# Cluster scores of an attention kernel: from twelve split-float products per head to four plain fp32 products in column groups

## The chip, the cores and the metric

The kernel runs on one core of one Trainium2 chip. The metric is the device time of one execution in microseconds; the time before is a median of 3 runs. The engines are TensorE (PE in the rows, with PEld for its weight loads), VectorE (DVE), ScalarE (ACT), GpSimd (POOL) and SyncE (SP, which only issues transfers here; GpSimd issues transfers too).

## The reference, cut to what matters

The whole reference is an attention whose keys are masked by cluster, and behind it two mixture layers, of which the change touches nothing.

```python
q_n = q / (norm(q) + 1e-06); k_n = ...; c_n = ...       # q, k: (2, 8, 768, 64), centroids: (8, 16, 64)
q_assign = argmax(einsum('bhsd,hcd->bhsc', q_n, c_n))   # first of equal maxima
k_assign = argmax(einsum('bhsd,hcd->bhsc', k_n, c_n))
mask = q_assign[:, :, :, None] == k_assign[:, :, None, :]
scores = where(mask, matmul(q, k.T) / 8, -1e9)
attn = softmax(scores)
x = matmul(attn, v)                                     # then the two mixture layers on x
```

The cluster of a row is the centroid with the highest score among 16; the norm of the row itself doesn't matter for that.

## The kernel before, in words

There are 16 heads g (2 batches of 8), two query halves u per head, three blocks of 128 queries per half. The scores of a block are one step n. The attention is software-pipelined by slots: slot s issues the scores of step s + 4 (`S`, `s_mm`), their row maximum (`M`, `s_max`), an exponential (`E`, `s_exp`), two groups of three transposes of the probabilities of 384 queries (`T` and `t`, `transp`, L458) and their products with the values (`V` and `v`, `pv`). The order inside a slot is written out by hand:

```python
LEAD = 4
ORDER = "ESTLAtVMlvZB"
```

Everything else is put into the places `A`, `Z` and `B` of a slot by a table: `at(slot, "a", fn)` puts a function there, and `steps(base, when, gen)` runs one step of a generator at each of the places listed in `when`. "-13a" with base 6g is place A of the slot 13 before head g's slots; place A lies between the transposes `T` and `t` on TensorE. Each engine runs its own instructions strictly in the order in which this walk issues them, and waits at an instruction whose data is not there.

An operand of head g is `t1` (128 partitions, 2, 768): index j=0 are queries, j=1 keys. For j=0 partitions 0 to 63 hold the high part of the 64 features (fp32r) and 64 to 127 the low part, for j=1 the other way round, so that one product over 128 partitions gives the sum of both parts. A transfer of GpSimd fills t1 (L330), and `rest_qk` (L337, on GpSimd, one instruction for each j, 64x768) subtracts to make the low parts. Its two steps are issued at -19b and -15a for odd heads, at -19b and -15b for even ones, at -16b and -15b for head 3. Also on GpSimd are the sums and scalings of a finished pair of heads (`norm`, L552, L557, L563; a pair is finished every 12 slots, issued at 8b to 11z of the next pair), the split of the values (L351), transfers (L330, L331, L347), and the mask steps below. `t2` (80 partitions) holds the high parts again, and in rows 64 to 79 the one-hot of the cluster (for queries 0 or 1, for keys 0 or -2^60), which makes the mask part of the score product (L435).

`cluster(g)` makes these rows in 11 steps. Twelve products (L370; 128 rows of t1 stationary, 32 columns of centroids moving: 16 of their high and 16 of their low parts), the sum of both parts (L377 ScalarE, L379 VectorE), the row maximum (L381 VectorE), a difference, a scaling and a tie-break on GpSimd (L393 to L395), a second maximum (L397), a difference (L399 GpSimd), a one-hot (L401 ScalarE), six transposes of 64 columns (L405), a copy with the factor of queries or keys (L415 ScalarE) and two transfers of SyncE into t2 (L417). For heads 3 and up its steps stand at

```python
CL = ("-13a", "-13a", "-13a", "-13z", "-12z", "-12b", "-10a", "-10a", "-9a", "-9b", "-9b")
```

PSUM buffers with the tag "t" come from a ring of three banks (`ps_t`), which T, t and the cluster steps share.

Of the kernel before, what the change touches and what calls it, by code (L numbers as in the profile page):

```python
# [8 lines left out]
F32 = mybir.dt.float32  # L9
F32R = mybir.dt.float32r  # L10
BF16 = mybir.dt.bfloat16
I32 = mybir.dt.int32
U32 = mybir.dt.uint32
ACTF = mybir.ActivationFunctionType
ALU = mybir.AluOpType
AX = mybir.AxisListType
PSUM = bass.MemoryType.PSUM

B, H, S, D = 2, 8, 768, 64
NCL = 16  # L20
# [5 lines left out]
NQ = S // 128  # L26
NPAIR = H // 2
BIG = float(2.0 ** 60)
# [11 lines left out]
def tile_cluster_attention_moe(ctx, tc, qk, vt, cent, consts, wm1, wm2, probs, probs_t, out):  # L40
    nc = tc.nc
    V, A, G, T, SY = nc.vector, nc.scalar, nc.gpsimd, nc.tensor, nc.sync
# [9 lines left out]
    ident = const.tile([128, 128], F32, name="ident")  # L52
    wtie = const.tile([128, NCL], BF16, name="wtie")
    zero1 = const.tile([128, 1], F32, name="zero1")
    cT = const.tile([128, H, 2, NCL], F32R, name="cT")
    identb = const.tile([128, 128], BF16, name="identb")
# [229 lines left out]
    def attention():  # L286
        with ExitStack() as ax:
            qkp = ax.enter_context(tc.tile_pool(name="qkp", bufs=2))
            stg = ax.enter_context(tc.tile_pool(name="stg", bufs=1))
            clp = ax.enter_context(tc.tile_pool(name="clp", bufs=1))  # L290
# [4 lines left out]
            ps_t = ax.enter_context(tc.tile_pool(name="ps_t", bufs=3, space=PSUM))  # L295
            ps_v = ax.enter_context(tc.tile_pool(name="ps_v", bufs=1, space=PSUM))
# [4 lines left out]
            ops = {}  # L301
# [12 lines left out]
            def low_raw(g, j, eng):  # L314
                r = slice(64, 128) if j == 0 else slice(0, 64)
                t = ops[g]["t1"][r, j]
                eng.tensor_tensor(out=t, in0=ops[g]["raw"][j][r], in1=t.bitcast(F32), op=ALU.subtract)
# [31 lines left out]
            def rest_v(g):  # L349
                vs, vraw = ops[g]["vs"], ops[g]["vraw"]  # L350
                G.tensor_tensor(out=vs[:, :, 1], in0=vraw, in1=vs[:, :, 0].bitcast(F32), op=ALU.subtract)  # L351

            oh_t = [clp.tile([128, NQ, 2, 32], BF16, name=f"oh{h}") for h in range(2)]

            def cluster(g):


                N = 2 * NQ
                t1, t2 = ops[g]["t1"], ops[g]["t2"]
                oh = oh_t[g % 2]  # L360
                ohn = oh[:, :, :, :NCL]
                pc = (ps_v if g == 1 else ps_t).tile([128, N, 2, NCL], F32, tag="v" if g == 1 else "t", name="pc")
                sc = clp.tile([128, N, NCL], F32, tag="sc", name="sc")
                mx = clp.tile([128, N, 1], F32, tag="mx", name="mx", bufs=2)
                eq = clp.tile([128, N, NCL], BF16, tag="eq", name="eq", bufs=2)
                mw = clp.tile([128, N, 1], BF16, tag="mw", name="mw", bufs=2)
                wb = wtie.rearrange("p (o c) -> p o c", o=1).to_broadcast([128, N, NCL])
                for j in range(2):
                    for c in range(NQ):
                        T.matmul(  # L370
                            out=pc[:, 2 * c + j].rearrange("p a b -> p (a b)"),
                            lhsT=t1[:, j, c * 128:(c + 1) * 128],
                            rhs=cT[:, g % H].rearrange("p a b -> p (a b)"),
                            start=True, stop=True,
                        )
                    yield
                A.copy(out=sc, in_=pc[:, :, 1])  # L377
                yield
                V.tensor_tensor(out=sc, in0=pc[:, :, 0], in1=sc, op=ALU.add)  # L379
                yield  # L380
                V.tensor_reduce(out=mx, in_=sc, axis=AX.X, op=ALU.max)  # L381
                yield
                if g < 2:
                    V.tensor_tensor(out=eq, in0=sc, in1=mx.to_broadcast([128, N, NCL]), op=ALU.is_equal)
                    V.tensor_tensor(out=eq, in0=eq, in1=wb, op=ALU.mult)
                    yield
                    V.tensor_reduce(out=mw, in_=eq, axis=AX.X, op=ALU.max)
                    yield
                    V.tensor_tensor(
                        out=ohn, in0=eq.rearrange("p (c j) n -> p c j n", j=2),  # L390
                        in1=mw.rearrange("p (c j) n -> p c j n", j=2).to_broadcast([128, NQ, 2, NCL]), op=ALU.is_equal)
                else:
                    G.tensor_tensor(out=sc, in0=sc, in1=mx.to_broadcast([128, N, NCL]), op=ALU.subtract)  # L393
                    G.tensor_tensor(out=sc, in0=sc, in1=huge.rearrange("p (o c) -> p o c", o=1).to_broadcast([128, N, NCL]), op=ALU.mult)
                    G.tensor_tensor(out=sc, in0=sc, in1=wb, op=ALU.add)  # L395
                    yield
                    V.tensor_reduce(out=mx, in_=sc, axis=AX.X, op=ALU.max)  # L397
                    yield
                    G.tensor_tensor(out=sc, in0=sc, in1=mx.to_broadcast([128, N, NCL]), op=ALU.subtract)  # L399
                    yield  # L400
                    A.activation(out=ohn, in_=sc.rearrange("p (c j) n -> p c j n", j=2), func=ACTF.Relu, bias=1.0)  # L401
                yield
                pt = ps_t.tile([64, S], BF16, tag="t", name="pt")
                for c in range(NQ):
                    T.transpose(pt[:, c * 128:(c + 1) * 128], oh[:, c].rearrange("p j n -> p (j n)"), identb)  # L405
                yield
                if g < 3:
                    A.activation(out=t2[64:80, 1], in_=pt[32:48], func=ACTF.Copy, scale=BIG, bias=-BIG)
                    yield
                    for hs in (slice(0, 384), slice(384, S)):  # L410
                        A.copy(out=t2[64:80, 0, hs], in_=pt[0:16, hs])  # L411
                    yield
                else:
                    mk = clp.tile([64, S], F32, tag="mk", name="mk")
                    A.activation(out=mk, in_=pt, func=ACTF.Identity, scale=mkc[:, 0:1], bias=mkc[:, 1:2])  # L415
                    for j in range(2):
                        SY.dma_start(out=t2[64:80, j].bitcast(F32), in_=mk[32 * j:32 * j + 16])  # L417
                    yield

            P_t, rs_t, nm_t, pT, pv_t, xu_t, r_t = {}, {}, {}, {}, {}, {}, {}  # L420

# [148 lines left out]
            def at(slot, pos, fn):  # L570
                tasks.setdefault((slot, pos), []).append(fn)

            def steps(base, when, gen):
                for w in when:
                    at(min(base + int(w[:-1]), NS - 1), w[-1], lambda: next(gen, None))
# [5 lines left out]
            def lazy(make, *args):  # L581
                yield from make(*args)
# [5 lines left out]
            V.memset(zero1, 0.0)  # L588
            huge = clp.tile([128, 1], F32, name="huge")
            V.memset(huge, HUGE)  # L590
            mkc = clp.tile([64, 2], F32, name="mkc")
            for j, v in enumerate((1.0, 0.0, BIG, -BIG)):
                V.memset(mkc[j // 2 * 32:j // 2 * 32 + 32, j % 2:j % 2 + 1], v)

            def warm(n):

# [8 lines left out]
            load_raw(1)  # L605
            load_raw(2)
            setup, head = consts_setup(clp, ps_t), cluster(0)
            warm(11)
            next(setup)
# [47 lines left out]
            for p in range(P - 1):  # L657
                steps(12 * (p + 1), ("1a", "2z", "2b", "5a"), recip(p))
                steps(12 * (p + 1), ("8b", "9z", "10a", "10z", "11z"), norm(p, G))
            CL = ("-13a", "-13a", "-13a", "-13z", "-12z", "-12b", "-10a", "-10a", "-9a", "-9b", "-9b")  # L660
            CL1 = ("-3a", "-3z", "-3b", "-2z", "-2b", "-1z", "-1z", "0z", "0b", "1a")
            CL2 = ("-10a", "-10a", "-10a", "-10z", "-9a", "-9a", "-8a", "-8a", "-8b", "-7z", "-7b", "-6a")
            steps(0, CL1, head)
            at(-1, "z", hold)
            for j in range(2):
                at(-1, "b", lambda j=j: low_raw(2, j, G))
            for g in range(NH):
                c = 6 * g
                if g > 3:
                    at(c - 23, "z", lambda g=g: load_qk(g))  # L670
                if g > 2:
                    steps(c, ("-16b", "-15b") if g == 3 else ("-19b", "-15a") if g % 2 else ("-19b", "-15b"), lazy(rest_qk, g, G))
                if g > 1:
                    steps(c, CL2 if g == 2 else CL, lazy(cluster, g))
                if g:
                    at(0 if g == 1 else c - 8, "z", lambda g=g: load_v(g))
                at(c - 4, "z", lambda g=g: rest_v(g))
# [16 lines left out]
            for slot in range(-LEAD, NS):  # L694
                n = slot + LEAD
                ready = slot >= 0
                if ready:
                    u, t = divmod(slot, 3)
# [41 lines left out]
    ct = {}  # L740
# [614 lines left out]
    with tc.manual_schedule():  # L1355
        attention()
        moe()
# [46 lines left out]
```

## Time and profile before

| | |
|---|---|
| median of 3 runs | 1037.88 us (1036.76 to 1038.18) |
| profiled execution | 1037.56 us, of which the span from first to last instruction is 1035.5 us |
| granted TensorE clock, mean | 0.995 of 2.4 GHz |
| attention stage | about 16 to 266 us of the span |
| busy share | PE 99%, PEld 81%, DVE 81%, ACT 61%, POOL 34% |

The profile is of one execution. A row of the timeline gives start and duration in us, the engine, the line, the operation, output and inputs, the count of equal instructions merged, and in brackets how long the engine was idle before it and what ended the wait. Matmuls are pipelined, so that a row's duration is longer than the time until the next one starts.

### The profile page before, as it was taken

The page shows a single profiled execution, that of the slowest core. Times are in us where ns is not written, and L with a number is a line of the kernel's source. Part 1 is how long each engine was busy: PE and PEld are TensorE (multiplying, and loading weights), DVE is VectorE, ACT ScalarE, POOL GpSimd, SP SyncE. Part 2 cuts the span into 40 slices and gives each one's busy share as a digit, 9 for nine tenths or more (in the row PEclk, how much of TensorE's full clock was granted, in tenths as well). Part 3 has the DMA queues.
Part 4 walks back from the last instruction along what each step waited for, and adds up shares of the span by engine and source line. Part 5 has one row for each costly group of instructions (what it writes and reads, how often), then busy time and mean ns, then how long its engine had stood idle before and what let it go on. Part 6 is the DMA issues. An engine that isn't in the chain of part 4 may idle for free.

```text
span 1035.5 us, 14784 instructions
## 1 busy us (share of the span) xinstructions
PE 1025.4 (99%) x5051; PEld 841.4 (81%) x5051; DVE 836.5 (81%) x1528; ACT 626.9 (61%) x1200; POOL 349.6 (34%) x395
## 2 busy tenths in 40 slices
PE   8999999999999999999999999999999999999998
PEld 5788888887788888788888888888888888888887
DVE  6788888898678887878687688898888888888875
ACT  6778878777467565645545656565555646555550
POOL 2747777652200101010100144433344443334430
PEclk8999999999999999999999999999999999999999
DMA  8677868832632624262410176755667665555753
GB/s 207 166 170 179 189 156 170 184 77 56 175 85 82 142 82 102 81 143 77 107 42 21 41 143 122 157 108 103 122 132 153 122 138 110 124 117 122 143 102 122
DMA packets 61267, 126.23 MB, mean 122 GB/s; under 512 B 15648, under 2 KB 20256, under 8 KB 61192
## 3 DMA queue, kind: packets, MB, share of 16 engines
q0 software_dynamic: 35632, 62.93, 33.1%
q1 hardware_dynamic: 25272, 62.30, 20.3%
q8 instruction: 39, 0.64, 0.3%
q14 instruction: 36, 0.29, 0.1%
q10 hardware_dynamic: 288, 0.07, 0.0%
HBM read 69.47 MB, written 3.21 MB: 70 GB/s over the span
## 4 chain that ended last, share of the span: by engine, by line
PE 95%; DVE 2%; ACT 2%; issue 0%; DMA 0%; SPq 0%; ACTq 0%; DVEq 0%
PE pa L900 19%; PE pb L275 14%; PE pd L1127 13%; PE pd L1253 9%; PE pb L1182 7%; PE ps L458 6%; PE ps L435 4%; PE pb L900 3%; PE ps L436 3%; PE pa L275 3%; PE pv L488 2%; PE pv L493 2%; PE pv L494 2%; PE pc L370 2%; PE pd L1297 2%; PE pu L275 1%
## 5 line engine op out<-in xcount | busy, mean ns | idle before, releaser
L1145 POOL DMA_DIRECT2D acc<-ev x84 | 74.1, 1019 | 169.1 <-ACT ev L1144 165.6
L441 DVE CUSTOM_DVE_ANT_0 junk<-ps,zero 128x768 bf16<-128x768 f32 x96 | 91.0, 948 | 14.4 <-PE ps L436 11.9
L452 ACT ACTIVATE P<-ps,nm 128x768 f32<-128x768 f32 x96 | 86.7, 903 | 12.4 <-DVE nm L441 12.1
L1259 POOL DMA_DIRECT2D acc<-ev x24 | 20.6, 858 | 202.0 <-ACT ev L1258 199.3
L275 PE MATMUL pb<-xh,wuh 128*128 128x512 f32 x216 | 85.4, 396 | 0.0
L275 PE MATMUL pb<-xh,wul 128*128 128x512 f32 x216 | 84.9, 393 | 0.0
L275 PE MATMUL pb<-xl,wuh 128*128 128x512 f32 x216 | 84.1, 389 | 0.0
L458 PE MATMUL ps<-ident,P 128*128 128x128 f32 x576 | 82.7, 275 | 0.0
L1138 DVE TENSOR_TENSOR acc<-pd,acc 128x512 f32<-128x512 f32 x112 | 75.5, 689 | 8.5 <-PE pd L1127 5.0
L477 DVE TENSOR_TENSOR lo<-ps,hi 128x384 fp32r<-128x384 f32 x128 | 69.3, 554 | 15.2 <-ACT hi L463 14.1
L1153 POOL DMA_DIRECT2D acc<-ev x56 | 48.6, 868 | 86.1 <-ACT ev L1152 47.8
L1012 ACT CAST hh<-snap 128x512 fp32r<-128x512 f32 x31 | 19.3, 622 | 94.5 <-DVE snap L1009 94.5
L435 PE MATMUL ps<-t 80*128 80x512 f32 x192 | 70.4, 367 | 1.4 <-ACT t L411 0.8
L463 ACT CAST hi<-ps 128x384 fp32r<-128x384 f32 x128 | 57.3, 479 | 21.1 <-PE ps L458 20.9
L458 PEld LDWEIGHTS ps<-ident,P 128*128 128x128 f32 x576 | 65.6, 141 | 1.4
L436 PE MATMUL ps<-t 128*128 128x512 f32 x192 | 62.2, 345 | 0.0
L900 PE MATMUL pa<-xsh,wuh 128*128 128x512 f32 x150 | 59.7, 398 | 0.1
L1152 ACT ACTIVATE ev<-pb,pn 128x512 f32<-128x512 f32 x56 | 38.5, 687 | 34.8 <-PE pb L1182 23.4
L900 PE MATMUL pa<-xsh,wul 128*128 128x512 f32 x150 | 59.0, 393 | 0.0
L900 PE MATMUL pa<-xsl,wuh 128*128 128x512 f32 x150 | 58.9, 393 | 0.0
L900 PE MATMUL pa<-xh,wuh 128*128 128x512 f32 x150 | 58.4, 390 | 0.0
L900 PE MATMUL pa<-xh,wul 128*128 128x512 f32 x150 | 58.4, 389 | 0.0
(276 smaller groups left out, 3136.5 us busy)
## 6 DMA issues: line engine op xcount, KB each, us to landing
acc<-ev POOLq DMA_DIRECT2D x164, 256.0 KB, 4.6
wraw<-in_wm SPq DMA_DIRECT2D x68, 512.0 KB, 3.8
t<-in_qk POOLq DMA_DIRECT2D x13, 768.0 KB, 6.3
t<-in_qk POOLq DMA_DIRECT2D x14, 384.0 KB, 7.8
raw<-in_qk SPq DMA_DIRECT2D x26, 192.0 KB, 7.0
x<-x SPq DMA_DIRECT2D x21, 192.0 KB, 2.8
R<-rd SPq DMA_DIRECT2D x16, 192.0 KB, 3.4
out<-acc SPq DMA_DIRECT2D x11, 256.0 KB, 2.0
```

The source lines that it names most:

```text
L275: T.matmul(out=ps, lhsT=w[:, o:o + 128], rhs=x, start=(k == 0 and m == 0), stop=(k == 3 and m == 2))
L435: T.matmul(out=ps, lhsT=t2[:, 0, qs], rhs=t2[:, 1, ks], start=True, stop=False)
L436: T.matmul(out=ps, lhsT=t1[:, 0, qs], rhs=t1[:, 1, ks], start=False, stop=True)
L441: V.tensor_tensor_reduce(out=junk, in0=S_t[n], in1=zero1.to_broadcast([128, S]), scale=-0.125, scalar=3.0e38, op0=ALU.add, op1=ALU.min, ac ...
L452: A.activation(out=P_t[n], in_=S_t.pop(n), func=ACTF.Exp, scale=0.125, bias=nm_t.pop(n), accum_out=rs_t[p][:, h, c:c + 1])
L458: T.transpose(ps[:, i * 128:(i + 1) * 128], P_t[3 * u + i][:, j * 128:(j + 1) * 128], ident)
L900: T.matmul(out=ps, lhsT=w[:, o:o + 128], rhs=r, start=first and i == 0 and m == 0, stop=i == 1 and m == 2, skip_group_check=not first)
L1127: T.matmul(out=ps[s], lhsT=w[i][:, o + s * 128:o + s * 128 + 128], rhs=x[j], start=first and m == 0, stop=m == 2, skip_group_check=not first)
L1138: V.tensor_tensor(out=y, in0=ps, in1=y, op=ALU.add)
L1145: G.dma_start(out=acc1[:, 2 * half + s, tb * 512:(tb + 1) * 512], in_=ev, accum_op=ALU.add)
L1182: T.matmul(out=ps, lhsT=h[i][:, f, ts_], rhs=w[j][:, f * DM + cs.start:f * DM + cs.stop], start=(f == 0 and m == 0), stop=(f == FC - 1 and ...
L1253: T.matmul(out=ps, lhsT=w[:, o:o + 128], rhs=x[:, f, sl], start=(n == 0), stop=(n == len(terms) - 1))
```

## The change

Heads 3 to 15 get a function of their own, `cluster4`. At its start the centroids stand still, 32 columns of them (16 of the head and 16 of a neighbour, which are dropped later), and four plain fp32 products of 384 moving columns write four groups of 32 partitions of one bank: queries and keys of the first and of the second half. Each plain fp32 product takes the sum of both parts of the centroids, which GpSimd adds once, in slot 2. ScalarE copies the scores (128x384), three fp32 transposes turn them, ScalarE copies the 16 wanted columns of each block, and from there the steps are those of before (`best`). The one-hots are turned in three transposes of 128 columns instead of six of 64; the mask copy is 128x384 instead of 64x768, and four transfers of 16x384 replace two of 16x768. The steps start one slot earlier: the products at -14a, the copy at -14z, transposes and second copy at -13a; from -12z on the places are the old ones. Heads 0 to 2 keep the products of before.

```diff
+            def best(g, sc):
+                oh = oh_t[g % 2]
+                mx = clp.tile([128, N2, 1], F32, tag="mx", name="mx", bufs=2)
+                V.tensor_reduce(out=mx, in_=sc, axis=AX.X, op=ALU.max)
+                yield
...
+                A.activation(out=oh[:, :, :, :NCL], in_=sc.rearrange("p (c j) n -> p c j n", j=2), func=ACTF.Relu, bias=1.0)
+                yield
...
+            def cluster4(g):
+                t1, t2 = ops[g]["t1"], ops[g]["t2"]
+                pc = ps_t.tile([128, 384], F32, tag="t", name="pc")
+                o = max(g % H - 1, 0) * NCL
+                cF = ct["cn"][:, o:o + 32]
+                o = g % H * NCL - o
+                for i in range(4):
+                    half, j = divmod(i, 2)
+                    T.matmul(out=pc[32 * i:32 * i + 32], lhsT=cF, rhs=t1[:, j, half * 384:half * 384 + 384].bitcast(F32),
+                             start=True, stop=True, skip_group_check=True)
+                yield
+                cs = clp.tile([128, 384], F32, tag="cs", name="cs")
+                A.copy(out=cs, in_=pc)
+                yield
+                ps = ps_t.tile([128, 384], F32, tag="t", name="pcT")
+                for c in range(3):
+                    T.transpose(ps[:, c * 128:(c + 1) * 128], cs[:, c * 128:(c + 1) * 128], ident)
+                yield
+                sc = clp.tile([128, N2, NCL], F32, tag="sc", name="sc")
+                A.copy(out=sc, in_=ps.rearrange("p (n c) -> p n c", c=32)[:, :, o:o + NCL])
+                yield
+                yield from best(g, sc)
+                pt = ps_t.tile([128, 384], BF16, tag="t", name="pt")
+                for c in range(3):
+                    T.transpose(pt[:, c * 128:(c + 1) * 128], oh_t[g % 2][:, 2 * c:2 * c + 2].rearrange("p i j n -> p (i j n)"), identb)
+                yield
+                mk = clp.tile([128, 384], F32, tag="mk", name="mk")
+                A.activation(out=mk, in_=pt, func=ACTF.Identity, scale=mkc[:, 0:1], bias=mkc[:, 1:2])
+                for i in range(4):
+                    half, j = divmod(i, 2)
+                    SY.dma_start(out=t2[64:80, j, half * 384:half * 384 + 384].bitcast(F32), in_=mk[32 * i:32 * i + 16])
+                yield
...
-            mkc = clp.tile([64, 2], F32, name="mkc")
-            for j, v in enumerate((1.0, 0.0, BIG, -BIG)):
-                V.memset(mkc[j // 2 * 32:j // 2 * 32 + 32, j % 2:j % 2 + 1], v)
+            mkc = clp.tile([128, 2], F32, name="mkc")
+            for i in range(4):
+                for j in range(2):
+                    G.memset(mkc[32 * i:32 * i + 32, j:j + 1], ((1.0, 0.0), (BIG, -BIG))[i % 2][j])
...
-            CL = ("-13a", "-13a", "-13a", "-13z", "-12z", "-12b", "-10a", "-10a", "-9a", "-9b", "-9b")
+            CL = ("-14a", "-14z", "-13a", "-13a", "-12z", "-12b", "-10a", "-10a", "-9a", "-9b", "-9b")
...
+            at(2, "z", lambda: G.tensor_tensor(out=ct["cn"].rearrange("p (h c) -> p h c", h=H), in0=cT[:, :, 0].bitcast(F32), in1=cT[:, :, 1].bitcast(F32), op=ALU.add))
...
-                    steps(c, CL2 if g == 2 else CL, lazy(cluster, g))
+                    steps(c, *((CL2, lazy(cluster, g)) if g == 2 else (CL, lazy(cluster4, g))))
```

## Rows read from the trace of the kernel before

**Rows 1.** The page: busy time by engine, and the chain that ended last.

```profile
PE 1025.4 (99%) x5051; PEld 841.4 (81%) x5051; DVE 836.5 (81%) x1528; ACT 626.9 (61%) x1200; POOL 349.6 (34%) x395
...
PE 95%; DVE 2%; ACT 2%; issue 0%; DMA 0%; SPq 0%; ACTq 0%; DVEq 0%
```

**Rows 2.** Timeline of TensorE, 109 to 116 us (start us, us, engine, line).

```profile
109.84 0.54 PE L488 MATMUL pv<-hi,vn 128*64 128x384 f32 x1
109.84 0.54 PE L488 MATMUL pv<-pT,vn 128*64 128x384 f32 x1
...
110.53 0.50 PE L405 MATMUL pt<-identb,oh 128*64 128x128 bf16 x6
110.96 0.50 PE L435 MATMUL ps<-t 80*128 80x512 f32 x1
...
111.77 0.82 PE L458 MATMUL ps<-ident,P 128*128 128x128 f32 x6
112.35 0.42 PE L493 MATMUL pv<-hi,vs 128*128 128x384 f32 x1
...
114.09 1.49 PE L370 MATMUL pc<-cT,t 128*128 128x32 f32 x12
115.43 0.55 PE L458 MATMUL ps<-ident,P 128*128 128x128 f32 x3
```

**Rows 3.** Timeline of TensorE's weight loads, at head 3's products and at 110 us.

```profile
37.52 1.41 PEld L370 LDWEIGHTS pc<-cT,t 128*128 128x128 f32 x12 [0.17 <-POOL t L337]
...
109.83 0.13 PEld L488 LDWEIGHTS pv<-hi,vn 128*64 128x64 f32 x1 [0.17 <-issue]
```

**Rows 4.** Groups of instructions of ScalarE (busy us, mean ns, idle before), 26 to 250 us.

```profile
L463 ACT CAST hi<-ps 128x384 fp32r<-128x384 f32 x118 | 52.8, 479 | 16.9 <-PE ps L458 16.7 <-ACT hi L463 0.2
...
L415 ACT ACTIVATE mk<-pt,mkc 64x768 f32<-64x768 bf16 x13 | 12.9, 993 | 3.7 <-PE pt L405 3.7
```

**Rows 5.** Timeline of GpSimd: second L337 of heads 3, 6, 7, 8, 14; first mask step.

```profile
35.68 1.84 POOL L337 TENSOR_TENSOR t<-raw,t 64x768 fp32r<-64x768 f32 x1
...
82.25 1.85 POOL L337 TENSOR_TENSOR t<-raw,t 64x768 fp32r<-64x768 f32 x1
...
93.62 1.82 POOL L337 TENSOR_TENSOR t<-raw,t 64x768 fp32r<-64x768 f32 x1
...
104.68 0.52 POOL L393 TENSOR_TENSOR sc<-sc,mx 128x192 f32<-128x192 f32 x1 [3.13 <-DVE mx L381]
...
112.45 1.84 POOL L337 TENSOR_TENSOR t<-raw,t 64x768 fp32r<-64x768 f32 x1
...
203.05 1.84 POOL L337 TENSOR_TENSOR t<-raw,t 64x768 fp32r<-64x768 f32 x1
```

**Rows 6.** Timeline of VectorE: the row maximum of head 7's cluster scores.

```profile
104.17 0.34 DVE L381 TENSOR_REDUCE mx<-sc 128x12 f32<-128x192 f32 x1
```

**Rows 7.** Timeline of TensorE: transposes at -14 of five heads; head 6's first scores.

```profile
35.03 0.82 PE L458 MATMUL ps<-ident,P 128*128 128x128 f32 x6
...
81.47 0.82 PE L458 MATMUL ps<-ident,P 128*128 128x128 f32 x6
...
96.28 0.82 PE L458 MATMUL ps<-ident,P 128*128 128x128 f32 x6
...
106.31 0.39 PE L435 MATMUL ps<-t 80*128 80x512 f32 x1
...
141.97 0.82 PE L458 MATMUL ps<-ident,P 128*128 128x128 f32 x6
...
202.37 0.82 PE L458 MATMUL ps<-ident,P 128*128 128x128 f32 x6
```

**Rows 8.** Timeline of SyncE's queue: the two mask transfers of head 6.

```profile
96.59 1.19 SPq L417 DMA_DIRECT2D t<-mk  x2
```

**Rows 9.** All mask transfers (L417): from issue to landing.

```profile
DMA to landing us min/median/max: 2.1/3.4/6.7
```

**Rows 10.** One stretch: busy us by engine (instructions), PE clock, DMA share, GB/s.

```profile
193.00:196.50 3.50, 2.72 (x15) 1.76 (x15) 2.89 (x7) 3.29 (x9) 1.06 (x3) 1.00 0.69 174
```

More of the change, by code (lines that the diff above doesn't have):

```diff
@@ L351, in rest_v @@
                 G.tensor_tensor(out=vs[:, :, 1], in0=vraw, in1=vs[:, :, 0].bitcast(F32), op=ALU.subtract)
+            N2 = 2 * NQ
+            wb = wtie.rearrange("p (o c) -> p o c", o=1).to_broadcast([128, N2, NCL])
             oh_t = [clp.tile([128, NQ, 2, 32], BF16, name=f"oh{h}") for h in range(2)]
+            def best(g, sc):
[3 more added lines that the diff above has]
+                yield
+                G.tensor_tensor(out=sc, in0=sc, in1=mx.to_broadcast([128, N2, NCL]), op=ALU.subtract)
+                G.tensor_tensor(out=sc, in0=sc, in1=huge.rearrange("p (o c) -> p o c", o=1).to_broadcast([128, N2, NCL]), op=ALU.mult)
+                G.tensor_tensor(out=sc, in0=sc, in1=wb, op=ALU.add)
+                yield
+                V.tensor_reduce(out=mx, in_=sc, axis=AX.X, op=ALU.max)
+                yield
+                G.tensor_tensor(out=sc, in0=sc, in1=mx.to_broadcast([128, N2, NCL]), op=ALU.subtract)
+                yield
+                A.activation(out=oh[:, :, :, :NCL], in_=sc.rearrange("p (c j) n -> p c j n", j=2), func=ACTF.Relu, bias=1.0)
+                yield
             def cluster(g):
-                N = 2 * NQ
                 t1, t2 = ops[g]["t1"], ops[g]["t2"]
@@ L361, in cluster @@
                 ohn = oh[:, :, :, :NCL]
[L362 to L367, printed above, removed]
+                pc = (ps_v if g == 1 else ps_t).tile([128, N2, 2, NCL], F32, tag="v" if g == 1 else "t", name="pc")
+                sc = clp.tile([128, N2, NCL], F32, tag="sc", name="sc")
                 for j in range(2):
@@ L380, in cluster @@
                 yield
-                V.tensor_reduce(out=mx, in_=sc, axis=AX.X, op=ALU.max)
-                yield
                 if g < 2:
-                    V.tensor_tensor(out=eq, in0=sc, in1=mx.to_broadcast([128, N, NCL]), op=ALU.is_equal)
+                    mx = clp.tile([128, N2, 1], F32, tag="mx", name="mx", bufs=2)
+                    eq = clp.tile([128, N2, NCL], BF16, tag="eq", name="eq", bufs=2)
+                    mw = clp.tile([128, N2, 1], BF16, tag="mw", name="mw", bufs=2)
+                    V.tensor_reduce(out=mx, in_=sc, axis=AX.X, op=ALU.max)
+                    yield
+                    V.tensor_tensor(out=eq, in0=sc, in1=mx.to_broadcast([128, N2, NCL]), op=ALU.is_equal)
                     V.tensor_tensor(out=eq, in0=eq, in1=wb, op=ALU.mult)
@@ L391, in cluster @@
                         in1=mw.rearrange("p (c j) n -> p c j n", j=2).to_broadcast([128, NQ, 2, NCL]), op=ALU.is_equal)
+                    yield
                 else:
[L393 to L402, printed above, removed]
+                    yield from best(g, sc)
                 pt = ps_t.tile([64, S], BF16, tag="t", name="pt")
@@ L406, in cluster @@
                 yield
[L407 to L418, printed above, removed]
+                A.activation(out=t2[64:80, 1], in_=pt[32:48], func=ACTF.Copy, scale=BIG, bias=-BIG)
@@ new lines, in cluster @@
+                yield
+                for hs in (slice(0, 384), slice(384, S)):
+                    A.copy(out=t2[64:80, 0, hs], in_=pt[0:16, hs])
+                yield
+            def cluster4(g):
[8 more added lines that the diff above has]
+                             start=True, stop=True, skip_group_check=True)
+                yield
+                cs = clp.tile([128, 384], F32, tag="cs", name="cs")
+                A.copy(out=cs, in_=pc)
+                yield
+                ps = ps_t.tile([128, 384], F32, tag="t", name="pcT")
+                for c in range(3):
+                    T.transpose(ps[:, c * 128:(c + 1) * 128], cs[:, c * 128:(c + 1) * 128], ident)
+                yield
+                sc = clp.tile([128, N2, NCL], F32, tag="sc", name="sc")
+                A.copy(out=sc, in_=ps.rearrange("p (n c) -> p n c", c=32)[:, :, o:o + NCL])
+                yield
+                yield from best(g, sc)
+                pt = ps_t.tile([128, 384], BF16, tag="t", name="pt")
+                for c in range(3):
+                    T.transpose(pt[:, c * 128:(c + 1) * 128], oh_t[g % 2][:, 2 * c:2 * c + 2].rearrange("p i j n -> p (i j n)"), identb)
+                yield
+                mk = clp.tile([128, 384], F32, tag="mk", name="mk")
[3 more added lines that the diff above has]
+                    SY.dma_start(out=t2[64:80, j, half * 384:half * 384 + 384].bitcast(F32), in_=mk[32 * i:32 * i + 16])
+                yield
```

## Prediction, made before the change was run

> **What bounds the kernel now.** I read the page first: TensorE is busy for 99% of the span, and 95% of the chain that ended last is TensorE's [rows 1]. So a microsecond taken from TensorE's stream counts, and so does a microsecond for which it is made to wait; work on the other engines counts only through such waits. Then I read TensorE's timeline in the attention stage, where the change lies, to see what the old products and turns take from one start to the next, which is their price on the bound engine [rows 2], and its weight loads, which show what the next product waited for [rows 3]. Last I read GpSimd's timeline over the same slots, since GpSimd finishes the operand that the moved products read [rows 5].
>
> **What is removed from TensorE.** The old scores of one head are 12 products. In the slot read here the first starts at 114.09 and the transposes behind them at 115.43, so they hold TensorE for 1.34 us. The six one-hot turns go from 110.53 to 110.96, 0.43 us [rows 2]. Together 1.77 us for each of 13 heads.
>
> **What is added to TensorE.** The four fp32 products with 32 stationary columns have no row of their own. The nearest are the two fp32 products of 384 columns with 64 stationary columns (L488), which write different halves of the output's partitions. Both start at 109.84, and what follows starts at 110.53 [rows 2], so two groups ran side by side in 0.69 us. Ahead of them the weight load stood 0.17 us for "issue" [rows 3]. From below: four groups side by side and no entry gap, 0.69 us. From above: four in a row, 4 x 0.69 + 0.17 = 2.93 us. I take 0.86 us, four side by side with the gap, since the row shows groups running together and nothing in it ties that to two.
> The Trainium skill (TensorE: Matmul & The Clock Gate, Part 3, "Measured speedup vs the span model") speaks a little against this: three column tiles of 32 gave a speedup of 2.38, not 3, so a pack costs more than one product. By that figure, as an estimate, 3 / 2.38 = 1.26 times 0.69 us is 0.87 us, with the gap 1.04 us, and the end of the sum below would be 2.3 us later. The trace of before has only two tiles (L488) and can't decide it.
> The three fp32 transposes of the scores go by L458, six of which go from 111.77 to 112.35 [rows 2], 0.097 us each: 0.29 us. The three bf16 one-hot turns go at the old 0.43 / 6 = 0.072 us each: 0.22 us; should a stationary side twice as wide make them as dear as the fp32 ones, 0.29 us.
> New sum: 0.86 + 0.29 + 0.22 = 1.37 us against 1.77, so 0.40 us less per head and **5.2 us less in 13 heads**, if nothing waits.
>
> **What the other engines get.** ScalarE loses half of the mask copy (0.99 us for 768 columns) and gains a copy of 128x384, which by L463 is 0.48 us [rows 4]: even. VectorE loses an addition. SyncE issues four mask transfers instead of two: the two took 1.19 us to issue from 96.59 [rows 8], so two more make it about 2.4 us, to 99.0; with the longest landing seen, 6.7 us [rows 9], that is 105.7, and the first scores of that head (6) start at 106.31 [rows 7]. So it is hidden, by only 0.6 us in the worst landing and by some 4 in the usual one; were it late, scores would wait by that much. Behind these issues on SyncE stand the loads of the next values and operands, about 1.2 us later, which are asked for several slots ahead. GpSimd's one extra addition (slot 2) stands in a stretch in which it waits for a transfer; the small sets of the constants move to GpSimd before anything there is due. Both at nothing; if the cover is gone, well under 1 us, once. The three-bank ring gets one allocation more per head, but the turned scores' bank waits only for a ScalarE copy issued a whole slot before.
>
> **What is moved, and this decides.** The products go from -13a to -14a, one slot earlier. Their rows come from t1, and the half of t1 for the keys is finished by the second L337 of the head on GpSimd. For even heads this L337 is issued at -15b, just ahead. But it does not run then, since GpSimd is behind its program there: it waits for the first row maximum of the odd head before (VectorE, starting at 104.17 [rows 6]), and then runs without a break from 104.68 through mask steps, operand transfers, the value split and the sums of the finished pair, with L337 the last, 112.45 to 114.29 [rows 5]. In the old kernel the key half was first read 0.67 us after 114.09, that is at 114.76: 0.47 us to spare. At -14a it is wanted a slot earlier. The transposes of that slot start at 111.77 [rows 2], and three of them later, at 112.06, the new products come. The second product (keys, first half) then waits until 114.29: **2.23 us**. TensorE takes its products in order, so behind it stand the other two products, three transposes, the value products and the next scores; ScalarE and VectorE then run dry.
> This falls on every even head whose L337 stands behind the sums of a pair, which are heads 6, 8, 10, 12 and 14, five in all. For the first, L337 ends at 84.10 [rows 5] and the place is 81.47 + 0.29 = 81.76 [rows 7]: 2.34 us. For the last, 204.89 against 202.37 + 0.29: 2.23 us. With 2.22 for each of the other two: **11.2 us**. Head 4 has no pair ahead of it.
> Odd heads have L337 two positions earlier and behind no sums: head 7's ends at 95.44 [rows 5], and its place is 96.28 + 0.29 = 96.57 [rows 7], 1.1 us to spare, so they get no wait.
> Head 3 has both halves late: its L337 runs 35.68 to 37.52 [rows 5], and the old products waited 0.17 us for it [rows 3]. The new place is 35.03 + 0.29 = 35.32 [rows 7]: 2.20 us, 2.0 of them new.
> Does the wait heal itself? No: the next one is counted again from a maximum that follows TensorE's own progress. From head 8's place (112.06) to head 10's (141.97 + 0.29 = 142.26 [rows 7]) is 30.2 us now. GpSimd's stretch is 9.6 us (104.68 to 114.29) and ends 2.2 us after the place, so from a place to the start of the next stretch it is 30.2 + 2.2 - 9.6 = 22.8 us. After the change a period is that, less what two heads save before the maximum (0.80 less the odd head's turn of 0.21: 0.6 us), plus the stretch: 31.8 us, 1.6 us more per pair with all saving in it. Two small corrections cancel: the odd head's turn lies after the maximum and what it saves only lengthens the wait (0.21 x 5); the entry gap is spent inside the wait (0.17 x 6).
>
> **The sum.** -5.2 + 11.2 + 2.0 = +8.0 us. Against the profiled execution (1037.56 us, of which 1035.5 is the span) that is 1045.6, and the median of the runs is 0.3 above that execution: **1046 us**.
>
> **Rivals.**
> *No wait, and faster.* If GpSimd reaches L337 about 2.2 us sooner relative to TensorE, the 13 us go and 5.2 us of saving remain: 1032.5 us. For it: GpSimd's chain begins with VectorE's maximum, and VectorE loses an addition just ahead. Against it: that maximum stands in VectorE's program behind a row maximum over scores of the same slot, so it can't come 2.2 us earlier. From the point where the wait per even head is under about 0.6 us the change is faster. 0.14.
> *A smaller wait.* The maximum comes about 1 us earlier, and each wait is 1.2 us: -5.2 + 6 + 2 = +2.8, about 1040.5 us. 0.09.
> *The four groups don't run together.* Two and two: 0.69 us more for 13 heads, less what hides in the waits, about +8 on the forecast: 1054 us. One by one, 2.07 us more each: about 1070 us. For it: the trace shows only two groups together. Against it: they show no hindrance at all. 0.08 and 0.05.
> *The clock.* A wait could cost more if TensorE's clock fell. In the stretch 193 to 196.5, where TensorE was busy 2.72 of 3.50 us, it was granted 1.00 [rows 10], that is 2.4 GHz. So no price.
>
> **Chances.** The forecast (1042 to 1050 for its own range) has 0.64, the smaller wait 0.09, groups two by two 0.08, one by one 0.05, no wait 0.14. The range of 1038 to 1055 holds the first three. What this kernel's measurement can tell from no change is about 0.2%, 2.1 us. Faster by more: 0.15 (no wait, and a sliver of the smaller wait); within: 0.05, the low half of the smaller wait; slower: 0.80.
>
> **What the profile after should show.** Four products and the next transposes starting 0.86 us apart where nothing waits (odd heads); three transposes 0.29 us a slot later; one-hot turns 0.22 us. In the waits of TensorE's loads, the new scores line behind GpSimd's second subtraction of the operand, six times, with the first of the four products started and the others some 2 us behind; TensorE's idle in the attention stage up by 8 to 13 us, and nothing moved after it. The forecast is wrong if the second L337 of heads 6 to 14 ends before the products' place, if products of different groups start 0.3 us or more apart, or if scores wait for a mask transfer.

## The result, and the profile after

The changed kernel took 1045.15 us (median of 4 runs, 1044.18 to 1047.78) where the kernel before took 1037.93 us: a ratio of 1.0076 (95% interval 1.0054 to 1.0097). That is 7.2 us slower by the two medians and 7.9 by the ratio. Its profiled execution has a span of 1042.5 us, 7.0 us more than the 1035.5 us before.

The page's busy times, and the chain that ended last, of the kernel after, answer to [rows 1]:

```profile
PE 1025.4 (98%) x4999; PEld 826.6 (79%) x4999; DVE 835.0 (80%) x1511; ACT 628.8 (60%) x1213; POOL 350.1 (34%) x404
...
PE 86%; POOL 5%; DVE 2%; DMA 2%; issue 1%; ACT 1%; SPq 1%; POOLq 0%; ACTq 0%; DVEq 0%
```

TensorE is busy as long as before to the tenth, in 52 instructions fewer; TensorE's part of the chain fell from 95% to 86%, and GpSimd, which was not on the chain's list before, has 5%. The busy time alone doesn't show a saving, because products that overlap count once and a product issued early into a wait counts in full. The waits have to be read.

In the kernel after, the new products are L432, the copies of the scores L436 and L443, the transposes of the scores L440 and of the one-hots L448, the mask transfers L454. L472 and L473 are the scores (L435, L436 before), L495 the transposes of the probabilities (L458), L525 the fp32 value products (L488), L589, L594, L598 and L600 the steps of the finished pair (L552, L557, L561, L563). L337 is still the subtraction on GpSimd.

TensorE's timeline of the kernel after around the products of head 4 (nothing waits), head 6 and its turned scores, and a one-hot turn, answers to [rows 2, 7]:

```profile
50.17 0.34 PE L448 MATMUL pt<-identb,oh 128*128 128x128 bf16 x3
50.32 0.48 PE L472 MATMUL ps<-t 80*128 80x512 f32 x1
...
51.12 0.49 PE L495 MATMUL ps<-ident,P 128*128 128x128 f32 x3
51.54 0.85 PE L432 MATMUL pc<-t,cn 128*32 128x384 f32 x8
52.32 0.55 PE L495 MATMUL ps<-ident,P 128*128 128x128 f32 x3
...
80.79 0.83 PE L432 MATMUL pc<-t,cn 128*32 128x384 f32 x2
83.08 0.85 PE L432 MATMUL pc<-t,cn 128*32 128x384 f32 x6 [1.46 <-POOL t L337]
83.86 0.55 PE L495 MATMUL ps<-ident,P 128*128 128x128 f32 x3
...
85.98 0.49 PE L440 MATMUL pcT<-ident,cs 128*128 128x128 f32 x3
86.31 0.49 PE L495 MATMUL ps<-ident,P 128*128 128x128 f32 x3
```

Each plain fp32 product is two records, so four products are eight. In head 4 all eight stand in one group that lasts 0.85 us, and the next instruction starts 0.78 us after their first. In head 6 the first product (queries, first half) goes at 80.79; the other six records start at 83.08, after 1.46 us of idle that GpSimd's L337 ended. From the first product to the next transposes it is 3.07 us instead of 0.78: the wait costs 2.29 us. The same two rows stand at 112.83 and 115.12, 144.39 and 146.72, 176.22 and 178.53, 208.05 and 210.34 (heads 8 to 14), and at 33.41 and 35.47 for head 3.

GpSimd's timeline of the kernel after, at the same place, answers to [rows 5]:

```profile
77.54 1.82 POOL L589 TENSOR_TENSOR x<-x,x 128x768 f32<-128x768 f32 x1
79.44 1.83 POOL L594 TENSOR_TENSOR x<-x,R 128x768 f32<-128x768 f32 x1
81.23 1.80 POOL L337 TENSOR_TENSOR t<-raw,t 64x768 fp32r<-64x768 f32 x1
```

L337 begins only 0.44 us after the first product and ends at 83.03; the second product starts at 83.08.

TensorE's waits for weight loads in the stage from 26 to 250 us, kernel after (us in total, times, longest):

```profile
PEld pc L432 <- POOL t L337: 12.7, 6, 2.2
PEld L448 <- ACT oh L371: 7.8, 13, 0.6
PEld ps L472 <- ACT hi L500: 7.8, 13, 0.6
...
PEld pc L432 <- issue: 2.2, 13, 0.2
```

Six waits for L337, 12.7 us, stand where before there was one of 0.17 us [rows 3]; the others lie mostly under running products. The mixture layers behind the stage take as long as before.

### The profile page after: what moved, and what is told of

It reads as the page before. It is cut to its first block, busy times and chain, and to the rows that moved or that the text cites. A ratio compares the mean times of both kernels' runs of the same rounds, so it can differ in the third digit from the quotient of the medians.

```text
span 1042.5 us, 14735 instructions
## 1 busy us (share of the span) xinstructions
PE 1025.4 (98%) x4999; PEld 826.6 (79%) x4999; DVE 835.0 (80%) x1511; ACT 628.8 (60%) x1213; POOL 350.1 (34%) x404
## 4 chain that ended last, share of the span: by engine, by line
PE 86%; POOL 5%; DVE 2%; DMA 2%; issue 1%; ACT 1%; SPq 1%; POOLq 0%; ACTq 0%; DVEq 0%
PE pa L939 19%; PE pb L275 14%; PE pd L1166 13%; PE pd L1292 9%; PE pb L1221 7%; PE ps L495 4%; PE pb L939 3%; PE pa L275 3%; DMA raw<-in_qk 2%; PE ps L472 2%; PE pd L1336 2%; PE ps L473 2%; PE pv L530 2%; PE pv L531 2%; PE pv L525 1%
## 5 line engine op out<-in xcount | busy, mean ns | idle before, releaser
L495 PE MATMUL ps<-ident,P 128*128 128x128 f32 x576 | 85.1, 275 | 0.0
L495 PEld LDWEIGHTS ps<-ident,P 128*128 128x128 f32 x576 | 65.9, 141 | 9.8 <-issue 3.8
L472 PE MATMUL ps<-t 80*128 80x512 f32 x192 | 69.6, 362 | 1.5 <-ACT t L419 0.8
L473 PE MATMUL ps<-t 128*128 128x512 f32 x192 | 61.7, 342 | 0.0
```

Source lines behind the costliest of these rows:

```text
L472: T.matmul(out=ps, lhsT=t2[:, 0, qs], rhs=t2[:, 1, ks], start=True, stop=False)
L473: T.matmul(out=ps, lhsT=t1[:, 0, qs], rhs=t1[:, 1, ks], start=False, stop=True)
L495: T.transpose(ps[:, i * 128:(i + 1) * 128], P_t[3 * u + i][:, j * 128:(j + 1) * 128], ident)
```

## The experiments

Ten kernels ran, in three groups; each group has its own runs of the kernel before, on the same chip. "Stage" is the difference to the kernel before, in one profiled execution each, of the time from the start of head 2's products to the first product of the mixture layer (226.0 us before). In profiled executions head 2's products start anywhere from 26.07 to 29.53 us, so that the timed ratio decides and the stage only shows where.

| run | ratio to before (95% interval) | us by the ratio | stage, us |
|---|---|---|---|
| changed kernel | 1.0076 (1.0054 to 1.0097) | +7.9 | +9.0 |
| e1_slot_back | 0.9950 (0.9934 to 0.9967) | -5.2 | -5.9 |
| e2_old_early | 1.0196 (1.0175 to 1.0216) | +20.3 | +21.2 |
| e3_sub_first | 1.0056 (1.0038 to 1.0074) | +5.8 | +6.3 |
| e4_both | 1.0044 (1.0029 to 1.0060) | +4.6 | +6.0 |
| e5_pair_later | 0.9995 (0.9986 to 1.0004) | -0.5 | +0.5 |
| e6_no_waits | 0.9985 (0.9971 to 0.9999) | -1.6 | -0.1 |
| e7_keys_first | 1.0123 (1.0109 to 1.0138) | +12.7 | +13.9 |
| e8_early_free | 1.0073 (1.0055 to 1.0090) | +7.6 | +8.0 |
| e9_pair_only | 1.0011 (1.0000 to 1.0022) | +1.1 | +3.8 |
| e10_copies_later | 0.9980 (0.9970 to 0.9990) | -2.1 | -1.5 |

The theory: the products and turns are cheaper, and the slot they were moved to makes TensorE wait for GpSimd's L337. The first rival: the loss lies in the new steps themselves.

**The first four steps one slot back.**

```diff
-            CL = ("-14a", "-14z", "-13a", "-13a", "-12z", ...
+            CL = ("-13a", "-13z", "-12a", "-12a", "-12z", ...
```

> The changed kernel with its first four steps one slot later (products at -13a, copy at -13z, transposes and second copy at -12a; all else as changed). Theory (the loss is TensorE's wait for GpSimd's second subtraction): the waits of 2.3 us in heads 6, 8, 10, 12, 14 and of 2.0 us in head 3 shrink to 0.1 to 0.3 us each, and the saving of the new products and turns, 13 x 0.37 = 4.8 us, shows: about 1034 us. Rival (the loss lies in the new steps: two more ScalarE copies in the chain, one more bank of the ring, four mask transfers): it stays, 1043 us or more.

It took 1030.4 us where the kernel before took 1035.5, 0.50% less and 13 us under the changed kernel by the two ratios: the theory's side. The 5.2 us are just what the prediction had worked out as the saving, but they are not made of it alone (see the transposes and turns below). Of the waits for L337 on TensorE's weight loads two are left, 0.3 us in all:

```profile
PEld pc L432 <- POOL t L337: 0.3, 2, 0.2
```

In the five even heads the products still took 0.88 to 1.07 us to the next transposes instead of 0.78.

The new steps, the copies, the extra bank and the four transfers are all in this run, so they are not the loss. It is also faster than both kernels, and so the version to keep.

**The old products, one slot early.**

```diff
-            CL = ("-13a", "-13a", "-13a", "-13z", "-12z", ...
+            CL = ("-14a", "-14a", "-13a", "-13z", "-12z", ...
```

> The kernel before with only the old products moved from -13a to -14a. Theory (wait): the six products of the queries run first and hide 0.67 us, so each wait is 2.23 - 0.67 = 1.6 us in five even heads and about 1.4 us in head 3: 9.4 us slower, 1047 us. Rival (the new steps cost, not the place): no change, 1038 us.

Slower, as the theory says, but by 20 us, twice what the waits give. The waits themselves came as expected, 9.5 us together. TensorE's timeline of this run, head 6, and busy times by stretch behind the wait, the last line a stretch around head 12's wait (length; PE, PEld, DVE, ACT, POOL busy with instructions; PE clock; DMA share; GB/s):

```profile
86.23 0.82 PE L370 MATMUL pc<-cT,t 128*128 128x32 f32 x6
88.51 0.84 PE L370 MATMUL pc<-cT,t 128*128 128x32 f32 x6 [1.46 <-POOL t L337]
89.20 0.55 PE L458 MATMUL ps<-ident,P 128*128 128x128 f32 x3
...
88.50:92.00 3.50, 3.49 (x18) 3.30 (x19) 0.56 (x1) 1.78 (x4) 1.81 (x2) 0.68 0.59 108
92.00:95.00 3.00, 3.00 (x19) 2.91 (x19) 1.96 (x5) 1.60 (x4) 2.55 (x2) 0.81 0.29 66
95.00:98.00 3.00, 3.00 (x21) 2.14 (x19) 2.96 (x9) 2.17 (x6) 1.16 (x3) 1.00 0.01 3
...
175.00:200.00 25.00, 23.36 (x159) 19.90 (x158) 20.68 (x49) 19.14 (x45) 18.10 (x21) 1.00 0.65 150
```

From 86.23 to 89.20 it is 2.97 us instead of 1.34 [rows 2], so 1.63 us of wait, where 1.6 was expected. But behind it the granted clock was 0.68 and 0.81, that is 1.2 GHz for a part of the stretch and 2.4 for the rest. (1 - 0.68) x 3.5 + (1 - 0.81) x 3.0 = 1.7 us of work were lost there besides the wait. Over the windows of the stage (26 to 250 us, mean clocks 0.93, 1.00, 0.93, 0.98, 0.95, 0.93, 1.00, 0.96, 0.97) the same arithmetic gives 8.7 us, and with the 9.5 us of the waits 18 of the 20 to 21 us.

The run has a head to compare with. In head 12 TensorE had the same six products ahead of the wait and was idle for 1.44 us, and the clock did not fall. The first scores of the slots around heads 6 and 12, in the same run:

```profile
80.52 0.40 PE L435 MATMUL ps<-t 80*128 80x512 f32 x1
98.35 0.39 PE L435 MATMUL ps<-t 80*128 80x512 f32 x1
...
181.34 0.40 PE L435 MATMUL ps<-t 80*128 80x512 f32 x1
197.59 0.40 PE L435 MATMUL ps<-t 80*128 80x512 f32 x1
```

Six slots around head 6 took 17.83 us, and as long around heads 8, 10 and 14, whose waits were followed by a fall too; around head 12 they took 16.25. So a fall costs about 1.6 us here, as much as a wait.

In the kernel after, the idle gap is equally long, 1.46 us, and the clock stays at 1.00:

```profile
80.00:84.00 4.00, 2.54 (x16) 1.01 (x15) 2.10 (x5) 2.13 (x5) 3.77 (x3) 1.00 0.26 48
84.00:87.00 3.00, 3.00 (x23) 2.91 (x23) 1.69 (x4) 2.50 (x7) 1.45 (x1) 1.00 0.62 119
```

What TensorE ran just ahead of the gap differs: six products of 32 columns here, one plain fp32 product of 384 columns there. That this is the reason is not shown, since head 12's gap stands behind the same six products.

**The subtraction first; and head 3 late as well.**

```diff
-  ("-19b", "-15a") if g % 2 else ("-19b", "-15b"), lazy(rest_qk, g, G))
+  ("-19b", "-15a") if g % 2 else ("-19b", "-16a"), lazy(rest_qk, g, G))
```

The second run has in addition the steps of the first experiment (-13a, -13z, -12a, -12a) for head 3 alone.

> The changed kernel with the products left at -14a, and GpSimd's second subtraction of even heads issued at -16a, ahead of the sums of the finished pair, instead of -15b. Theory (wait): the five waits of even heads go, that of head 3 stays: 1037.9 - 4.8 + 1.9 = 1035 us; the sums of the pair come 1.8 us later and nobody waits for them. Rival (new steps): no gain, 1045 us.

> As the run before, and head 3 alone has its first steps one slot later. Theory (wait): all waits are gone and only the saving is left, 1037.9 - 4.8 = 1033 us. Rival (new steps): 1045 us.

Both missed: 5.8 and 4.6 us over the kernel before, where -3 and -5 were expected. By the intervals neither is clear of the changed kernel, so the times alone leave the rival standing; the rows show what happened. The waits of the even heads for L337 were gone, and another had come one slot later. TensorE's and ScalarE's timelines of the first of these runs, head 6:

```profile
80.86 0.85 PE L432 MATMUL pc<-t,cn 128*32 128x384 f32 x8
...
83.44 0.49 PE L495 MATMUL ps<-ident,P 128*128 128x128 f32 x3
84.92 0.55 PE L440 MATMUL pcT<-ident,cs 128*128 128x128 f32 x3 [0.99 <-ACT cs L436]
```

```profile
83.19 0.51 ACT L598 CAST xh<-x 128x384 fp32r<-128x384 f32 x1 [1.39 <-POOL x L594]
83.60 0.47 ACT L500 CAST hi<-ps 128x384 fp32r<-128x384 f32 x1
83.97 0.52 ACT L598 CAST xh<-x 128x384 fp32r<-128x384 f32 x1
84.39 0.48 ACT L436 COPY cs<-pc 128x384 f32<-128x384 f32 x1
```

The products ran at 80.86 without a wait, but the copy that the transposes need (L436, at -14z) stands on ScalarE behind the two copies of the finished pair (L598), the first of which idles 1.39 us for GpSimd's L594, which the moved subtraction made later by its 1.8 us. TensorE waited 0.99 us, in five heads 4.9 us. So the products at -14 depend on GpSimd twice in those heads. In the changed kernel the second wait is covered by the first.

**The pair's copies one slot later.** To test that, the second of those runs got

```diff
-                steps(12 * (p + 1), ("8b", "9z", "10a", "10z", "11z"), norm(p, G))
+                steps(12 * (p + 1), ("8b", "9z", "11a", "11z", "12z"), norm(p, G))
```

> The run with the subtraction first and head 3 late, and in addition the two ScalarE copies of the scaled pair and the subtraction behind them one slot later (11a, 11z, 12z instead of 10a, 10z, 11z), so that the copy of the new scores no longer stands behind them. Theory (the wait of 1 us for the scores' copy in five heads is ScalarE standing at the pair's copies): it goes, 5 us under that run, about the kernel before or up to 0.4% under it. Rival (the new scores' copy is late by itself): no change, 0.4% over the kernel before.

It came out 2.1 us under the kernel before, 6.7 us under the run without this edit: the wait of L440 for L436 is gone from its list of waits, which settles the second wait. With products that stay at -14 it is still 3 us short of the first experiment.

**The pair later, instead of the subtraction earlier.**

```diff
-                steps(12 * (p + 1), ("8b", "9z", "10a", "10z", "11z"), norm(p, G))
+                steps(12 * (p + 1), ("10b", "11z", "12a", "12z", "13z"), norm(p, G))
```

This edit went into the changed kernel, into the changed kernel with head 3 one slot back, into the kernel with the old products early, and alone into the kernel before.

> The changed kernel with the sums, scaling and copies of a finished pair issued two slots later (10b, 11z, 12a, 12z, 13z of the next pair instead of 8b, 9z, 10a, 10z, 11z); everything else as changed. Theory (two waits in a row: GpSimd's subtraction behind the sums, and ScalarE's copy of the new scores behind its two copies of the scaled pair): both go for the even heads, head 3's wait stays: 1037.9 - 4.8 + 1.9 = 1035 us, 0.3% under the kernel before. Rival (place -14 itself is too early for VectorE and the bank ring): no better than with the subtraction moved ahead, 1041 us.

> As the run before, and head 3's first four steps one slot later. Theory: no wait is left, 1037.9 - 4.8 = 1033 us, as the run with all products one slot back (0.5% under the kernel before). Rival: 1040 us.

> The kernel before with the old products at -14a, and the sums of a finished pair two slots later, so that only head 3 waits. Theory (waits, and the clock that falls after them, made the 20 us of the old products at -14a): 1 to 3 us over the kernel before, 1039 to 1041 us. Rival (the early place itself, through the bank ring and VectorE): most of the 20 us stays, 1050 us or more.

> The kernel before, whose only edit is that sums, scaling and copies of a finished pair are issued two slots later. Theory (that reordering has a price of its own: ScalarE's two copies at 12a and 12z then stand ahead of an exponential for which the next scores wait): 2 to 4 us over the kernel before. Rival (the reordering is free, so the 5 us by which the two earlier runs with it missed their expectation come from place -14): no change.

With it the changed kernel is 8.4 us faster than without by the two ratios, equal to the kernel before, and with head 3 late 1.6 us under it: the waits were the larger part of the loss, but that is 3.6 us short of the first experiment. The old products early lost 13 of their 20 us and kept 7.6, more than expected and less than the rival said. Alone, the edit costs 1.1 us, less than expected; its interval of 0 to 2.3 holds both the theory's lower end and the rival's nothing. So about 1 us may be the price of the reordering, and some 2.5 us stay with the early place itself, in the new kernel, a difference no larger than the intervals it is taken from; in the old one more, of which head 3 has a part: TensorE waited 1.7 us there for L337, and the mean clock from 26 to 50 us was 0.93, (1 - 0.93) x 24 = 1.7 us more. A part of what is left is again L337: with the pair's sums two slots later and head 3 late, heads 9 and 13, which had no wait before, took 1.47 and 1.48 us for their products instead of 0.78. What the rest is made of I didn't settle: in these runs TensorE's remaining waits are of 0.2 to 1.3 us, for the one-hot (L371), for VectorE's lows and for ScalarE, no two alike.

**Keys first, so that the whole wait is idle.**

```diff
-                for i in range(4):
+                for i in (1, 3, 0, 2):
```

> The changed kernel with the four products issued keys first (both halves), then queries, so that TensorE does nothing at all in the wait: idle about 2.3 us instead of 1.46 in six heads. Theory by waiting alone: the remaining products run side by side after the wait as before, so the time is that of the changed kernel, 1045 us (0.7% over the kernel before). Rival by the clock: the granted clock falls after these longer gaps as it did after those of the old products at -14a (0.68 to 0.81 for some 5 us), about 1.5 us more in each: 1053 us.

12.7 us over the kernel before, between the two expectations. Nothing ran in the wait; its end is the same, and three of the six waits (heads 3, 6 and 10) left the clock as it was, but behind the other three it fell. TensorE's products of head 12, and the stretch behind them:

```profile
178.94 0.87 PE L432 MATMUL pc<-t,cn 128*32 128x384 f32 x8 [2.23 <-POOL t L337]
...
180.00:183.00 3.00, 3.00 (x12) 2.81 (x11) 0.56 (x1) 2.17 (x5) 1.22 (x1) 0.50 0.61 110
```

0.50 is 1.2 GHz: 1.5 us lost in these three microseconds. Three windows of 25 us have a mean of 0.93 (100 to 125, 175 to 200, 200 to 225), 0.07 x 75 = 5.3 us, about the difference to the changed kernel (4.8 us by the two ratios). Six slots around heads 8, 12 and 14 took 18.20 to 18.25 us, around heads 6 and 10 16.65 and 16.67: again 1.6 us for each fall.

## Why the prediction was right

It said 1046 us (1038 to 1055), slower, by a wait of TensorE for GpSimd's second subtraction in heads 3, 6, 8, 10, 12 and 14. Measured: 1045.15 us, and six such waits in just these heads.

*The waits.* Predicted 2.34, 2.23, 2.22, 2.22, 2.23 us for the even heads, 11.2 together; measured, from the first product to the next transposes less the 0.78 us of an undisturbed head, 2.29, 2.29, 2.33, 2.30 and 2.28, together 11.5. Head 3: 2.20 predicted, 36.24 - 33.41 - 0.78 = 2.05 measured. Odd heads had no wait. The wait didn't heal: it came again with every pair, to 0.05 us the same.

*The four groups side by side.* Predicted 0.86 us with the gap; measured 0.78 us and a gap ahead. The transposes ahead go at 51.12 and would take 0.29 us, to 51.41; the products start at 51.54, so the gap is 0.13 us. Four groups take what two took: the two of L488 have 0.69 us to the next start [rows 2], and in the kernel after the two of L525 have 0.79 us ahead of scores. The estimate from the Trainium skill's speedup of 2.38 for three column tiles (TensorE: Matmul & The Clock Gate, Part 3, "Measured speedup vs the span model") was 0.87 us without the gap; the trace has 0.78.

*Transposes and turns.* Predicted 0.29 and 0.22 us; measured 0.33 (85.98 to 86.31) and 0.15 (50.17 to 50.32). By these rows a head takes 0.91 + 0.33 + 0.15 = 1.39 us against the 1.37 predicted, and 1.77 before. But the rows leave out what stands ahead of each piece. TensorE's rows for that, of the kernel before and then of the kernel after:

```profile
46.08 0.39 PE L435 MATMUL ps<-t 80*128 80x512 f32 x1
...
60.72 0.39 PE L435 MATMUL ps<-t 80*128 80x512 f32 x1
...
113.84 0.49 PE L458 MATMUL ps<-ident,P 128*128 128x128 f32 x3
```

```profile
45.83 0.40 PE L472 MATMUL ps<-t 80*128 80x512 f32 x1
...
49.37 0.54 PE L525 MATMUL pv<-hi,vn 128*64 128x384 f32 x1
...
60.23 0.40 PE L472 MATMUL ps<-t 80*128 80x512 f32 x1
```

From the value products ahead of the turns to the scores behind them it was 1.12 us before (109.84 to 110.96 [rows 2]) and is 0.95 after (49.37 to 50.32): the turns save 0.17 us, not 0.28, since they start 0.80 us behind the first value product where the old ones started 0.69 behind it. From the transposes ahead of the products to those behind them it was 1.59 us (113.84 to 115.43) and is 1.20 (51.12 to 52.32): 0.39 us saved. With the 0.33 us of the new transposes, 0.23 us per head are left of the 0.40 predicted, 3.0 us in 13 heads instead of 5.2. Six whole slots around head 4's products, in which TensorE is never idle in either kernel, say the same: 14.64 us before (46.08 to 60.72), 14.40 after (45.83 to 60.23).

So this term of the sum was mis-sized, and that the first experiment gained just the 5.2 us predicted is partly luck. Some 3 us of it are cheaper products and turns; the rest lies in other waits that went as well, most of it in the odd heads: six slots around their products took 14.92 to 16.24 us before and 14.47 to 14.81 in that run.

*The sum.* In the profiled stage 13.4 us of new waits (11.5 + 2.05 - 0.17) went with +9.0. Of the 4.4 us between them 3.0 are the saving, and 1.4 must lie in other waits that became shorter, for which the prediction had no term. The whole was 8.0 predicted and 7.2 measured; the waits were foreseen, but the saving set too high and the other waits left out work against each other, so the closeness of the whole is in part luck. What lies ahead of the stage was shorter in the profiled execution after (head 2's products start at 27.49 instead of 29.53) and differs from one execution to the next.

*What was costed at nothing.* SyncE's four transfers, the added sum on GpSimd and the one more bank cost nothing that shows: landings of the masks took 1.9 to 5.8 us, and no score waited for one in the kernel after. Two sentences were wrong, though. The bank of the turned scores was said to wait only for a ScalarE copy issued a whole slot before; in the even heads that copy stands behind the pair's copies, which wait for GpSimd, and when the first wait was taken away this one cost 1 us a head. And the clock was given no price from one stretch with a gap; that held for the changed kernel, but not for gaps behind smaller products or with no product at all.

## What to carry to other kernels

Moving a step earlier on a bound engine moves it towards every producer that had just been on time; look up each operand's last write and the spare time of each, by occurrence and not on the mean, since here one head in two had 0.5 us of spare time and the other more than a slot. When the first late producer is cured, read the waits again before expecting the whole: the next one in line (here a copy behind another engine's wait) had been covered by it. A saving on the bound engine and a move in time are two changes: run each alone. And price a step from a start ahead of it to a start behind it, since its own rows don't show what its neighbours lose.

## What the runs showed of the hardware

Idle gaps of equal length were not always followed by a fall of the granted clock. In the kernel after, none of the six gaps of 1.23 to 1.50 us was, and one plain fp32 product of 384 columns had run just before each. With the old products early, five of the six gaps of 1.21 to 1.46 us were, with six products of 32 columns just before each; the sixth, of 1.44 us, was not. With the keys first, three of the six gaps of 2.0 to 2.2 us were, with only transposes and scores before them. A fall cost about 1.6 us, read from six slots with and without one in the same run. What decides in a single gap these runs don't show.

The stage's start differs by the clock as well. In the kernel before and after, windows from the first microseconds:

```profile
4.00:8.00 4.00, 2.25 (x13) 1.10 (x11) 2.83 (x9) 2.79 (x5) 0.85 (x2) 1.00 1.01 379
8.00:12.00 4.00, 3.99 (x17) 2.59 (x17) 3.12 (x11) 2.89 (x7) 0.47 (x3) 0.54 1.22 292
12.00:16.00 4.00, 4.00 (x19) 2.66 (x18) 2.18 (x3) 3.29 (x6) 2.74 (x4) 0.50 1.11 255
```

```profile
4.00:8.00 4.00, 3.51 (x13) 1.89 (x12) 3.45 (x12) 3.20 (x5) 0.71 (x2) 1.00 1.02 365
8.00:12.00 4.00, 4.00 (x17) 2.66 (x17) 2.88 (x8) 2.67 (x7) 1.12 (x3) 1.00 1.29 298
```

Before, TensorE was busy 2.25 of the four microseconds from 4 to 8, waiting for the first operands, and the clock was 0.54 and 0.50 from 8 to 16 us; after, it was busy 3.51 of them and the clock stayed at 1.00. That is no effect of the change that I could show: the run with the subtraction first and head 3 late, whose start is that of the changed kernel, had 0.50 from 8 to 16 us too. It may be a part of the scatter of 1.4 to 6.9 us between runs of one kernel.
